# Decode attention with a gated MLP: the K and V caches loaded head by head, with the lines of a head dealt to the partitions in turn

## The chip, the core and the metric

One core of one Trainium2 chip runs the kernel. The metric is the device time of one execution in microseconds (us). Before the change it is 1299.86 us, the median of three runs (1299.61 to 1300.03).

## The reference, cut to what matters

Two tokens (B = 2, one query position each) attend to caches of 32 heads with 8192 positions of 128 float32 values. The result passes through an output projection and is multiplied by the SiLU of a small MLP.

```python
def _A_ref(x, k_cache, v_cache, wq, wo):          # k_cache, v_cache: (2, 32, 8192, 128)
    q = (lambda x, *d: x.transpose(*d))((x @ wq).reshape(B, Sq, H, Dh), 0, 2, 1, 3)
    scores = jnp.einsum("bhqd,bhkd->bhqk", q, k_cache) * (Dh ** -0.5)
    p = _softmax(scores, axis=-1)
    o = jnp.einsum("bhqk,bhkd->bhqd", p, v_cache)
    return (lambda x, *d: x.transpose(*d))(o, 0, 2, 1, 3).reshape(B, Sq, H * Dh) @ wo
...
x = A_x
xn = _layernorm(x, axis=-1)
s = _A_ref(xn, A_k_cache, A_v_cache, A_wq, A_wo)
g = _silu(_B_ref(xn, B_w1, B_b1, B_w2, B_b2))     # layernorm, 512 -> 1376, GELU, -> 512
return x + s * g
```

K and V together are 537 MB in the chip's memory (HBM), each byte used once. All other inputs are 22 MB.

## The kernel before

**Tiles.** The work goes through N = 32 pairs of heads, two heads (U = 2) at a time. The 8192 positions of a head are cut into 64 lines of KP = 128 positions; a line is 128 x 128 float32 values, 64 KB that lie together in HBM. A pair has 128 lines, and each of the 128 partitions of the on-chip memory holds one: the first head's 64 lines are on partitions 0 to 63, the second head's on 64 to 127, in the order in which they lie in HBM. `kf[n]` and `vf[n]` are the views of the caches for pair `n`, `[128 lines, 128 positions, 128 values]`.

**Buffers.** There are three of 8 MB: `KBUF[0]` and `KBUF[1]` (the tiles `big0` and `big1`) take the K of even and odd pairs, `VB` (`big2`) takes every V. At the start the weights of the query projection and of the MLP stand in `big1` and `big2`, at the end the output weights `wo` in `big2`; the last pair's V goes to `KBUF[0]`.

**A pair's way.** VectorE multiplies all of a K buffer by the query in place (`TENSOR_TENSOR`, 128x16384) and sums over the 128 values (`TENSOR_REDUCE`). TensorE moves the maximum of each head to where it is wanted, ScalarE takes the exponential into `PZ`, and TensorE multiplies `PZ` by V in 32 steps (in `weighted`) and gathers the result. Small matmuls that nothing reads (`unread`) lie in between.

**What sets the order.** Every engine runs its own program, and semaphores that are counted up and taken down tie them together. SyncE (SP in the profile) issues all large loads, in one queue: for each pair it takes `p_k` (K has been read, the buffer is free), issues the next K, takes `p_free` (V has been read), issues the next V. VectorE takes 16 counts of `d_k0` or `d_k1` before it starts on a K buffer (in `scores`), TensorE takes 16 of `d_v` ahead of V. A load adds 16 to its semaphore when all of it is in. The last K and the last V are loaded in two halves by positions (`HALVES`), each with its own semaphore, so that work can begin on the first half.

The lines of the profile carry little here: nearly every instruction is issued through one helper and stands under L51, takes of a semaphore under L45. Instructions are told apart by tiles.

## Time and profile before

| | |
|---|---|
| median of three runs | 1299.86 us |
| profiled execution | 1299.53 us |
| its span, first to last instruction | 1298.2 us |
| VectorE busy | 1135.7 us (87%) |
| TensorE busy, matmuls | 465.6 us (36%) |
| ScalarE busy | 81.1 us (6%) |
| DMA packets of the SP queue | 559.30 MB, 99.7% of 16 engines' span |
| mean rate from HBM | 431 GB/s |

The page divides the span into 40 slices and gives for each the busy share of every engine and of the 16 DMA engines in tenths, and the GB/s that they moved. It then gives the DMA queues and the chain of work that ended last, followed back from the last instruction. A row of the timeline has its start and its length in us, the engine, the operation with the tile written and the tiles read, and in brackets how long the engine had been idle before it and what ended that. A row of a stretch has its limits, its length, the busy time of each engine with the number of instructions, the granted clock of TensorE as a share of full speed, the busy share of the DMA engines and the GB/s. A row of the DMA issues has the tile and its source, the queue, how many, the size of one, and the median time from issue to landing.

### The profile page before, as it was taken

The numbers are of one execution on the slowest core, as the hardware profiler recorded it, in microseconds if no ns is written. First come the engines' busy times: TensorE is split into PE (matmuls) and PEld (weight loads), VectorE is DVE, ScalarE is ACT, GpSimd is POOL, SyncE is SP. The second block draws the span as 40 slices with busy tenths as digits, with TensorE's granted clock in tenths as the row PEclk, the third lists the DMA queues.
The fourth block names the chain that finished last, engine by engine and source line by source line (L and its number), as shares of the span: only waits on it lengthen the run. The fifth ranks groups of instructions, "written<-read, shape, count | busy, mean of one in ns | idle before, by whom it ended". The sixth has DMA issues, their size and how long they took to land. (4 is left out here: it accounts for less than half of the span.)

```text
span 1298.2 us, 7420 instructions
## 1 busy us (share of the span) xinstructions
PE 465.6 (36%) x2958; PEld 150.8 (12%) x2958; DVE 1135.7 (87%) x171; ACT 81.1 (6%) x279; POOL 2.3 (0%) x15
## 2 busy tenths in 40 slices
PE   3813343323334322433322343322334321333338
PEld 1201111001111000111100111100111100111103
DVE  2599999988889988889988888988888988888991
ACT  1200000000000000000000000000000000000000
POOL 0000000000000000000000000000000000000000
PEclk8757766666776566677656767656776666677659
DMA  9999999999999999999999999999999999999998
GB/s 412 436 426 442 430 430 436 426 446 426 438 430 424 446 426 442 430 430 436 426 446 426 438 430 424 446 426 444 428 432 434 426 446 426 438 430 424 432 436 360
DMA packets 11241, 559.37 MB, mean 431 GB/s; under 512 B 1264, under 2 KB 1536, under 8 KB 1892
## 3 DMA queue, kind: packets, MB, share of 16 engines
q1 hardware_dynamic: 11228, 559.30, 99.7%
q8 instruction: 3, 0.05, 0.0%
q14 instruction: 2, 0.02, 0.0%
q10 hardware_dynamic: 8, 0.01, 0.0%
HBM read 559.30 MB, written 0.00 MB: 431 GB/s over the span
## 5 line engine op out<-in xcount | busy, mean ns | idle before, releaser
L51 DVE TENSOR_TENSOR big<-big,bank 128x16384 f32<-128x16384 f32 (+1 forms) x33 | 551.2, 16704 | 73.2 <-DVEq L45 73.2
L51 DVE TENSOR_REDUCE sc<-big 128x128 f32<-128x16384 f32 (+1 forms) x33 | 551.2, 16703 | 4.8
L51 PE MATMUL bank<-big,PZ 128*8 128x512 f32 x2048 | 293.0, 736 | 632.1 <-PEq L45 632.1
L51 PEld LDWEIGHTS bank<-big,PZ 128*8 128x8 f32 x2048 | 60.5, 103 | 837.3 <-issue 837.3
L51 PE MATMUL bank<-Q,ident 128*128 128x512 f32 (+2 forms) x198 | 79.8, 514 | 0.3 <-issue 0.3
L51 ACT COPY o<-bank 128x512 f32<-128x512 f32 x33 | 19.3, 586 | 887.3 <-ACTq L45 875.9
L51 PE MATMUL bank<-ident,MX 128*1 128x128 f32 x32 | 9.8, 308 | 132.8 <-PEq L45 132.8
L51 PE MATMUL bank<-mod,o 128*128 128x2 f32 x256 | 32.8, 250 | 27.4 <-PEq L45 27.4
L51 PEld LDWEIGHTS bank<-mod,o 128*128 128x128 f32 x256 | 31.0, 191 | 55.4 <-issue 55.4
L51 PEld LDWEIGHTS bank<-Q,ident 128*128 128x128 f32 x198 | 34.8, 205 | 16.5 <-issue 16.5
L51 ACT ACTIVATE PZ<-sc,bias 64x128 f32<-64x128 f32 x64 | 25.5, 399 | 6.6 <-ACTq L45 6.2
L51 DVE TENSOR_REDUCE nm<-bank 1x2 f32<-1x128 f32 x32 | 8.9, 279 | 19.4 <-DVEq L45 19.4
L51 DVE TENSOR_TENSOR big<-big,mine 64x512 f32<-64x512 f32 (+1 forms) x2 | 4.5, 2278 | 21.2 <-ACT big L51 21.2
L51 PEld LDWEIGHTS bank<-ident,MX 128*1 128x1 f32 x32 | 2.5, 79 | 157.8 <-issue 157.8
L51 ACT COPY bias<-bank 128x1 f32<-128x1 f32 x32 | 5.1, 159 | 220.2 <-ACTq L45 220.2
L51 PE MATMUL bank<-big,sides 64*128 64x512 f32 x16 | 12.8, 972 | 3.7 <-DVE big L51 3.7
L51 PE MATMUL bank<-nm,srow 1*64 1x1 f32 x128 | 10.4, 218 | 8.9 <-PEq L45 7.1
L51 DVE TENSOR_REDUCE MX<-sc 128x1 f32<-128x128 f32 x32 | 9.2, 286 | 4.7
L51 PE MATMUL bank<-big,xnT 128*2 128x512 f32 x64 | 9.0, 727 | 10.3 <-DMA big<-in_A_wq_dram 10.3
L51 ACT ACTIVATION_READ_ACCUMULATOR PZ<-sc,bias x64 | 11.8, 185 | 0.0
L51 PE MATMUL bank<-big,on 128*17 128x512 f32 (+1 forms) x88 | 10.8, 569 | 0.9 <-DMA big<-in_A_wo_dram 0.8
L51 DVE SCALAR_TENSOR_TENSOR res<-bank,gate 128x128 f32<-128x128 f32 x1 | 0.3, 291 | 11.9 <-PE bank L51 11.9
(80 smaller groups left out, 83.8 us busy)
## 6 DMA issues: line engine op xcount, KB each, us to landing
big<-in_A_k_cache_dram SPq DMA_DIRECT2D x2, 4096.0 KB, 35.9
big<-in_A_v_cache_dram SPq DMA_DIRECT2D x2, 4096.0 KB, 35.8
big<-in_B_w_dram SPq DMA_DIRECT2D x1, 2752.0 KB, 10.2
big<-in_B_w_dram SPq DMA_DIRECT2D x1, 2560.0 KB, 52.1
big<-in_A_wo_dram SPq DMA_DIRECT2D x1, 2560.0 KB, 15.0
big<-in_A_wo_dram SPq DMA_DIRECT2D x1, 2048.0 KB, 19.5
big<-in_A_wo_dram SPq DMA_DIRECT2D x1, 1536.0 KB, 22.7
big<-in_A_wo_dram SPq DMA_DIRECT2D x1, 1024.0 KB, 24.8
```

Source lines behind the costliest of these rows:

```text
L51: ins = getattr(self.engines[eng], method)(*args, **kwargs)
```

## The change

Each load of a pair becomes two, one for each head. The views `kf` and `vf` get the dimensions `s` (the head of the pair), `e` (16) and `r` (4), where line 16 r + e of a head goes to partition 4 e + r of the head's 64. Before, line number and partition were the same. As the 64 partitions are divided into 16 groups of four, group e holds lines e, 16 + e, 32 + e and 48 + e; the first lines of all groups are 16 neighbours in HBM, and so are the second ones. The new `fill` issues the two loads. Who waits for a load waits for 32 counts. The sums over positions do not depend on the order of the lines, and K and V are dealt alike.

```diff
-    kf = kc.rearrange("b h s d -> (b h s d)").rearrange("(n p j d) -> n p j d", p=P, j=KP, d=DH)
-    vf = vc.rearrange("b h s d -> (b h s d)").rearrange("(n p j d) -> n p j d", p=P, j=KP, d=DH)
+    kf = kc.rearrange("b h s d -> (b h s d)").rearrange("(n s r e j d) -> n s e r j d", s=U, e=16, j=KP, d=DH, n=N)
+    vf = vc.rearrange("b h s d -> (b h s d)").rearrange("(n s r e j d) -> n s e r j d", s=U, e=16, j=KP, d=DH, n=N)
...
+    def fill(buf, src, name, c0=0, c1=KP, waits=()):
+        for s in range(U):
+            op("SP", "dma_start", buf[HP * s:HP * (s + 1), c0:c1], src[s][:, :, c0:c1], sig=name, waits=waits)
+
     def load_k(n, *waits):
         sems, cuts = ([f"d_k{n % U}", "d_kl"], HALVES) if n == N - 1 else ([f"d_k{n % U}"], (0, KP))
         for name, (c0, c1) in zip(sems, zip(cuts, cuts[1:])):
-            op("SP", "dma_start", KBUF[n % U][:, c0:c1], kf[n][:, c0:c1], sig=name, waits=waits)
+            fill(KBUF[n % U], kf[n], name, c0, c1, waits)
...
             take("SP", "p_k")
-            op("SP", "dma_start", KBUF[u], kp[i + 1, u], sig=f"d_k{u}")
+            fill(KBUF[u], kp[i + 1, u], f"d_k{u}")
             take("SP", "p_free")
-            op("SP", "dma_start", VB, vp[i, 1] if not u else vp[i + 1, 0], sig="d_v")
+            fill(VB, vp[i, 1] if not u else vp[i + 1, 0], "d_v")
...
     for i, (c0, c1) in enumerate(zip(HALVES, HALVES[1:])):
-        op("SP", "dma_start", KBUF[N % U][:, c0:c1], vf[N - 1][:, c0:c1], sig=f"d_v31{i}")
+        fill(KBUF[N % U], vf[N - 1], f"d_v31{i}", c0, c1)
...
-            take("DVE", name, 16)
+            take("DVE", name, 16 * U)
...
-            take("PE", "d_v", 16)
+            take("PE", "d_v", 16 * U)
...
-                nc.tensor.wait_ge(pr.sem(f"d_v31{HALVES.index(i * JW)}"), 16)
+                nc.tensor.wait_ge(pr.sem(f"d_v31{HALVES.index(i * JW)}"), 16 * U)
```

On SP, in the body of the loop over pairs, stood one load for each turn of a buffer. A row has the tile and its source and the destination's shape, an `ISA` row is a take of a semaphore or a step of it:

```order
L51 ISA
L51 DMA big0<-in_A_k_cache_dram 128x16384
L51 ISA
L51 DMA big2<-in_A_v_cache_dram 128x16384
L51 ISA
L51 DMA big1<-in_A_k_cache_dram 128x16384
L51 DMA big2<-in_A_v_cache_dram 128x16384
```

Now the same place on SP reads:

```order
L51 ISA
L51 DMA big0<-in_A_k_cache_dram 64x1x16384
L51 ISA
L51 DMA big0<-in_A_k_cache_dram 64x1x16384
L51 ISA
L51 DMA big2<-in_A_v_cache_dram 64x1x16384
L51 ISA
L51 DMA big2<-in_A_v_cache_dram 64x1x16384
L51 ISA
L51 DMA big1<-in_A_k_cache_dram 64x1x16384
L51 ISA
L51 DMA big1<-in_A_k_cache_dram 64x1x16384
L51 DMA big2<-in_A_v_cache_dram 64x1x16384 x2
```

Each load of 128 partitions has become two of 64, one directly behind the other in the same queue, first the lower partitions, then the upper ones. The order on the other engines is as it was.

## The prediction

> **What bounds the kernel now.** I read the page first: which resource is full in every slice, and what ended last.

> ```profile
> DMA  9999999999999999999999999999999999999998
> ...
> DMA packets 11241, 559.37 MB, mean 431 GB/s; under 512 B 1264, under 2 KB 1536, under 8 KB 1892
> ...
> q1 hardware_dynamic: 11228, 559.30, 99.7%
> ...
> DMA big<-in_A_wo_dram 2%; PE bank L51 0%; SPq L51 0%; DVE res L51 0%; DVEq L50 0%
> ```

> The 16 DMA engines are busy in every slice, 99.7% of the span, and the last thing waited for is a load. So the kernel is as long as its bytes are. VectorE has 87% in the page's first part and looks like a second bound; the timeline of one steady pair of heads shows how it really stands. Here are VectorE's rows, then TensorE's, then SP's issues:

> ```profile
> 424.05 17.22 DVE L51 TENSOR_TENSOR big<-big,bank 128x16384 f32<-128x16384 f32 x1 [2.80 <-DVEq L45]
> 441.42 17.22 DVE L51 TENSOR_REDUCE sc<-big 128x128 f32<-128x16384 f32 x1
> ...
> 462.75 17.22 DVE L51 TENSOR_TENSOR big<-big,bank 128x16384 f32<-128x16384 f32 x1 [2.84 <-DVEq L45]
> ```

> ```profile
> 443.40 9.27 PE L51 MATMUL bank<-big,PZ 128*8 128x512 f32 x64 [21.63 <-PEq L45]
> 453.56 1.02 PE L51 MATMUL bank<-mod,o 128*128 128x2 f32 x8 [0.88 <-PEq L45]
> ```

> ```profile
> 383.15 0.33 SPq L51 DMA_DIRECT2D big<-in_A_k_cache_dram  x1
> 416.02 0.33 SPq L51 DMA_DIRECT2D big<-in_A_v_cache_dram  x1
> 421.97 0.33 SPq L51 DMA_DIRECT2D big<-in_A_k_cache_dram  x1
> 454.07 0.33 SPq L51 DMA_DIRECT2D big<-in_A_v_cache_dram  x1
> ...
> 532.03 0.33 SPq L51 DMA_DIRECT2D big<-in_A_v_cache_dram  x1
> ```

> VectorE starts a K buffer at 424.05, TensorE a V buffer at 443.40, VectorE the next K at 462.75: something lands every 19.35 us, one load behind the other. Each of the two engines stands idle just ahead of its start (2.84 us on VectorE, 21.63 on TensorE), so both wait for loads. The loads do not wait for them: V is issued at 416.02, 8.0 us before the K load ahead of it is through (424.05), and the next K at 421.97, while that V has still to run. The queue is never empty.

> Sizes and landing times are in the part on issues; the whole loads are two such halves:

> ```profile
> big<-in_A_k_cache_dram SPq DMA_DIRECT2D x2, 4096.0 KB, 35.9
> big<-in_A_v_cache_dram SPq DMA_DIRECT2D x2, 4096.0 KB, 35.8
> ...
> big<-in_A_k_cache_dram SPq DMA_DIRECT2D x31, 40.7
> big<-in_A_v_cache_dram SPq DMA_DIRECT2D x31, 27.9
> ```

> One load is 8192 KB = 8.389 MB. From the V issue at 416.02 to the one at 532.03 three pairs of loads pass: 116.01 / 3 = 38.67 us for 16.777 MB, 433.9 GB/s, or 19.33 us for a load. The 64 loads of K and V take 64 x 19.33 = 1237 us of the profiled execution's 1299.53 us (its span is 1298.2; the runs' median, 1299.86, is 0.33 above, which I neglect). Some 62 us are left for the weights, the start and the end.

> **Is there something to gain in the reading?** If memory set the rate, neighbouring addresses could help, and one would expect the rate to move with the place read. Six stretches of three pairs each, start to start:

> ```profile
> 416.02:532.03 116.01, 38.92 (x250) 12.27 (x250) 104.92 (x13) 6.47 (x24) 0.00 (x0) 0.66 1.00 433
> 532.03:648.18 116.15, 39.03 (x252) 12.45 (x251) 105.06 (x13) 6.47 (x24) 0.00 (x0) 0.66 1.00 433
> ...
> 996.35:1112.50 116.15, 38.79 (x252) 12.49 (x251) 105.07 (x13) 6.47 (x24) 0.00 (x0) 0.66 1.00 433
> ```

> ```profile
> 21.00:40.00 19.00, 9.04 (x64) 1.65 (x64) 0.74 (x5) 0.26 (x3) 0.00 (x0) 0.64 1.00 435
> ```

> Through 700 us of the caches the period stays at 116.00 to 116.16 us, and in the stretch from 21 to 40 us, with other addresses, the last column reads 435 GB/s. This is a fixed ceiling, not a memory that answers better or worse. Even at 435 everywhere 1237 us shrink by 0.25%, 3 us. So the reading order is worth 0 to -3 us, and I take 0.

> **The change part by part.**

> *The lines' order.* Every line is still 64 KB in one piece and goes to one partition; sums over the lines do not depend on their order, as K and V are dealt alike. Nothing on VectorE, TensorE or ScalarE is added or moved: 0 us.

> *Twice as many loads.* 66 whole or half loads become 132. Each issue takes SP 0.33 us (the rows above), 66 x 0.33 = 22 us in all on SP's queue, which waits most of the time. V's second piece is issued some 0.4 us after the first, 7.6 us ahead of need instead of 8.0: hidden by the K load in progress. K is issued 21 us ahead of need. What the 16 engines need to close a load with its signal has no row of its own, but small loads of the output weights, issued one behind the other, bound it:

> ```profile
> 1266.60 3.65 SPq L51 DMA_DIRECT2D big<-in_A_wo_dram  x8
> ...
> big<-in_A_wo_dram SPq DMA_DIRECT2D x1, 1024.0 KB, 24.8
> big<-in_A_wo_dram SPq DMA_DIRECT2D x1, 512.0 KB, 25.6
> big<-in_A_wo_dram SPq DMA_DIRECT2D x1, 256.0 KB, 25.7
> ```

> Issued 3.65 / 8 = 0.46 us apart, the second lands 1.26 us after the first, the third 0.56 after the second. Their bytes alone need 1.21 and 0.60 us at 433.9 GB/s. Closing a load therefore costs 0.05 us at most: 66 x 0 to 0.05 = 0 to 3 us. I take 0.5.

> *Both halves awaited.* VectorE and TensorE wait for 32 counts in place of 16. They start when the second half is in, which is when the whole load would have been: 0 us.

> *64 partitions at a time.* This is the term that decides. Every large load of before is 128 partitions wide. A load of one head writes partitions 0 to 63 only, and the next one 64 to 127, behind it in the same queue. The order of instructions shows the destination as 64 rows and the source as 16 neighbouring lines, so all 16 engines can take part, four lines each. What is the ceiling of 433.9 GB/s, then? If it is what the 16 engines can carry (27.1 GB/s each), a half takes 9.67 us and the pair of halves 19.33: 0 us. If it is what the partitions can take in (433.9 / 128 = 3.39 GB/s each, in groups that share an entrance), 64 of them take 217 GB/s, two engines stand at each entrance, and a half takes 19.33 us: the 64 loads take 1237 us more. Both readings fit every row, as no large row has another number of engines or of partitions. The one narrower load, 96 partitions, is too small to tell (192 KB in 4.1 us, nearly all of it the way to the first byte):

> ```profile
> big<-in_B_w_dram SPq DMA_DIRECT2D x1, 192.0 KB, 4.1
> ```

> So the bounds are 0 and +1237 us. I take the upper end, less a little. What all rows have in common is the full width of 128 partitions; no row shows 64 of them taking in more than their half of the rate, and the loads come strictly one after the other, so the two halves do not fill each other's gap. Less a little: where the engines are not quite level, the first ones are already writing the other half; at one issue's 0.33 us for each of 128 borders that is 42 us. It is an estimate. The compute cannot get in the way: VectorE's 104.92 / 3 = 35.0 us a pair fit twice into 77.

> The sum: 1299.5 + 1237 - 42 + 0.5 = **2,495 us**.

> [...]

> **The rivals.**

> *Not slower: the engines are the ceiling.* Place: the same term. For it: 433.9 GB/s is equally 16 times 27.1, and the stretches are as even as an engine's own clock would make them. Against it: nothing in the rows. It decides as soon as an entrance takes more than two engines bring, 54 GB/s. Then the time is 1299.5 + 0.5 = 1,300 us, within 0.2%, which is about what a measurement of this kernel can tell from no change.

> *Partly slower: the engines fall out of step.* At half rate a pair of engines shares an entrance only while both are in the same half. If one gets ahead by a whole half (four lines, 9.67 us of its own time), they write different halves and the loss is gone. The queue holds one to two loads, so such a lead has room, but the queue then runs about 2 us short before each V issue (8.0 us ahead of need against 9.67). With a share f of the time in step the time is 1300 + 1237 f: 1,920 us at one half. For it: nothing holds the engines level. Against it: nothing in the rows pushes them apart either, and every short queue lets the rear catch up.

> *Faster by neighbouring reads.* Bounded above at 3 us: 1,297 us. [...]

> **How the numbers follow.** Half the rate throughout, 2,495 us: 0.45, with a range of its own from 2,400 to 2,545 (1299.5 + 1237 + 3 and a few us more). Partly out of step, 1,303 to 2,400: 0.24. Engines as the ceiling, no change: 0.25. Slightly slower by a late V alone, up to 1,330: 0.03. Faster: 0.03. Slower is 0.45 + 0.24 + 0.03 = 0.72. The two ends hold so much each that the range has to span both: 1,297 to 2,545.

> **What would show it.** In the profile after: at half rate the GB/s of the slices falls to some 220 in the steady part, while the DMA share stays full; a K or V half lands every 19 us, VectorE's idle ahead of its multiply grows from 2.8 to some 40 us, and the issues on SP lie 77 us apart. If the engines are the ceiling, every one of these stays, with 0.33 us rows doubled on SP. Out of step, the rate starts near 220 and climbs from slice to slice. The prediction is wrong if the rate stays above 300 GB/s.

## The result: twice the time

The changed kernel takes 2636.28 us (median of six runs, 2618.94 to 2653.71) against 1299.82 us before (1299.61 to 1300.43): a ratio of 2.029, 95% interval 2.025 to 2.034. The direction and the halved rate of the forecast held, its size did not: 2,495 us was said and 2,545 us was the top of the range. The profiled execution took 2618.94 us.

The page after, with the lines that answer to those of before: the slices' busy shares and rates, the queue, the chain.

```profile
span 2617.2 us, 7584 instructions
...
DVE  2735553345533355433555334554335553345550
...
DMA  9999999999999999999999999999999999999997
GB/s 300 230 208 209 211 208 211 210 211 211 209 209 210 209 210 212 211 209 209 210 210 212 213 209 211 208 211 215 210 211 210 212 212 211 210 213 215 209 215 212
...
q1 hardware_dynamic: 12284, 559.30, 99.4%
...
DMA big<-in_A_wo_dram 2%; PE bank L51 0%; SPq L51 0%; DVE res L51 0%; DVEq L50 0%
```

The busy share of the DMA engines is as full as before (99.4% against 99.7%), and a load still ends the chain. What has changed stands one line below: from the third slice on the same busy engines move 208 to 215 GB/s in place of some 434. A busy share says that packets are on their way, not how fast.

The steady part, first VectorE's timeline (start, length, and in brackets the idle time ahead), then two rows of TensorE between them in time, then SP's issues:

```profile
760.79 17.22 DVE L51 TENSOR_TENSOR big<-big,bank 128x16384 f32<-128x16384 f32 x1 [26.45 <-DVEq L45]
778.16 17.22 DVE L51 TENSOR_REDUCE sc<-big 128x128 f32<-128x16384 f32 x1
795.52 0.29 DVE L51 TENSOR_REDUCE MX<-sc 128x1 f32<-128x128 f32 x1
813.42 0.28 DVE L51 TENSOR_REDUCE nm<-bank 1x2 f32<-1x128 f32 x1 [17.61 <-DVEq L45]
841.07 17.22 DVE L51 TENSOR_TENSOR big<-big,bank 128x16384 f32<-128x16384 f32 x1 [27.37 <-DVEq L45]
```

```profile
800.89 8.53 PE L51 MATMUL bank<-big,PZ 128*8 128x512 f32 x64 [66.12 <-PEq L45]
...
812.99 0.27 PE L51 MATMUL bank<-ident,MX 128*1 128x128 f32 x1
```

```profile
250.04 1.18 SPq L51 DMA_DIRECT2D big<-in_A_v_cache_dram  x2
253.55 1.28 SPq L51 DMA_DIRECT2D big<-in_A_k_cache_dram  x2
329.60 1.26 SPq L51 DMA_DIRECT2D big<-in_A_v_cache_dram  x2
...
410.65 1.18 SPq L51 DMA_DIRECT2D big<-in_A_v_cache_dram  x2
```

VectorE's work is the same (17.22 us each), but it starts a K buffer every 80.28 us, not every 38.7. Its idle time is spread over two places: 26 to 27 us ahead of the multiply (K is not in) and 18 us ahead of `nm`. For `nm` it needs TensorE, which works off the V of the pair before first; that V is late too, so the matmul with `MX` begins only at 812.99. From 250.04 to 410.65 us two pairs pass: 80.3 us a pair for 16.777 MB, 209 GB/s.

One more number, from the trace's packets, carries the rest of this text. A line of 64 KB is one packet (each of the two traces has 7,936 of 65,536 bytes for the K and V that are loaded whole), and its duration is recorded. The table has the lines of K and V that are loaded whole:

| kernel | mean of a line, us | median, us |
|---|---|---|
| before | 2.422 | 2.422 |
| after | 4.975 | 5.032 |

Before, 8.389 MB in 128 lines over 16 engines are 8 x 2.42 = 19.4 us, the time of a load. Now each engine needs more than twice as long for the same line. Twice 2.418, the fastest of before, would be 4.84.

### The profile page after: what moved, and what is told of

Same layout as the page of the kernel before. It is cut to its first block, busy times and chain, and to the rows that moved or that the text cites. A ratio compares the mean times of both kernels' runs of the same rounds, so it can differ in the third digit from the quotient of the medians.

```text
span 2617.2 us, 7584 instructions
## 1 busy us (share of the span) xinstructions
PE 451.6 (17%) x2958; PEld 147.5 (6%) x2958; DVE 1135.8 (43%) x171; ACT 81.0 (3%) x279; POOL 2.3 (0%) x15
## 3 DMA queue, kind: packets, MB, share of 16 engines
q1 hardware_dynamic: 12284, 559.30, 99.4%
HBM read 559.30 MB, written 0.00 MB: 214 GB/s over the span
## 5 line engine op out<-in xcount | busy, mean ns | idle before, releaser
L51 DVE TENSOR_TENSOR big<-big,bank 128x16384 f32<-128x16384 f32 (+1 forms) x33 | 551.2, 16704 | 816.6 <-DVEq L45 816.6
L51 PE MATMUL bank<-big,PZ 128*8 128x512 f32 x2048 | 289.3, 728 | 2055.5 <-PEq L45 2038.4
L51 DVE TENSOR_REDUCE sc<-big 128x128 f32<-128x16384 f32 (+1 forms) x33 | 551.2, 16703 | 4.8
L51 DVE TENSOR_REDUCE nm<-bank 1x2 f32<-1x128 f32 x32 | 8.9, 279 | 575.8 <-DVEq L45 575.8
L51 PEld LDWEIGHTS bank<-big,PZ 128*8 128x8 f32 x2048 | 59.6, 102 | 2258.0 <-issue 2240.1
L51 ACT COPY o<-bank 128x512 f32<-128x512 f32 x33 | 19.3, 585 | 2305.6 <-ACTq L45 2295.7
L51 PE MATMUL bank<-Q,ident 128*128 128x512 f32 (+2 forms) x198 | 75.0, 495 | 0.3 <-issue 0.3
L51 PE MATMUL bank<-mod,o 128*128 128x2 f32 x256 | 32.8, 250 | 27.4 <-PEq L45 27.4
L51 PEld LDWEIGHTS bank<-mod,o 128*128 128x128 f32 x256 | 31.0, 191 | 55.4 <-issue 55.4
L51 PEld LDWEIGHTS bank<-Q,ident 128*128 128x128 f32 x198 | 32.4, 191 | 27.2 <-issue 27.2
L51 ACT ACTIVATE PZ<-sc,bias 64x128 f32<-64x128 f32 x64 | 25.5, 399 | 6.6 <-ACTq L45 6.2
L51 DVE TENSOR_TENSOR big<-big,mine 64x512 f32<-64x512 f32 (+1 forms) x2 | 4.5, 2279 | 22.4 <-ACT big L51 22.4
L51 PE MATMUL bank<-big,sides 64*128 64x512 f32 x16 | 12.9, 980 | 3.7 <-DVE big L51 3.7
L51 PE MATMUL bank<-ident,MX 128*1 128x128 f32 x32 | 8.8, 276 | 20.8 <-PEq L45 20.8
L51 ACT ACTIVATION_READ_ACCUMULATOR PZ<-sc,bias x64 | 11.8, 184 | 0.0
L51 DVE TENSOR_REDUCE MX<-sc 128x1 f32<-128x128 f32 x32 | 9.1, 286 | 4.7
L51 PE MATMUL bank<-nm,srow 1*64 1x1 f32 x128 | 9.0, 196 | 11.6 <-PEq L45 11.6
L51 PE MATMUL bank<-big,xnT 128*2 128x512 f32 x64 | 8.9, 721 | 11.5 <-DMA big<-in_A_wq_dram 11.5
L51 DVE RECIPROCAL rl<-bank 128x2 f32<-128x2 f32 x1 | 0.2, 170 | 23.0 <-PE bank L51 23.0
L51 PE MATMUL bank<-big,on 128*17 128x512 f32 (+1 forms) x88 | 9.1, 484 | 1.0 <-DMA big<-in_A_wo_dram 0.9
L51 ACT COPY bank<-Q 128x128 f32 (+1 forms) x34 | 9.1, 269 | 0.8
L51 PE MATMUL bank<-big,hT 128*2 128x512 f32 (+1 forms) x22 | 5.3, 1049 | 17.4 <-DMA big<-in_B_w_dram 17.4
## 6 DMA issues: line engine op xcount, KB each, us to landing
big<-in_A_wo_dram SPq DMA_DIRECT2D x1, 1024.0 KB, 42.0
```

The costliest lines, as they stand in the source:

```text
L51: ins = getattr(self.engines[eng], method)(*args, **kwargs)
```

## The experiments

**Theory "entrance".** A supposition, drawn up to be tested: the engines share their ways into the partitions, called entrances here, one of which passes about what one engine brings; partitions 0 to 63 have half of them, to go by the rates (209 against 434 GB/s), so that two engines stand at each. Entrances stand in no row; what the runs can show is the rate and the time of a line for each choice of partitions and of source. **Rivals:** "reading" (16 neighbouring lines at a time come out of HBM slowly), "count" (twice as many loads cost it), "width" (the rate goes by the number of partitions of a load, wherever they lie), and for the 100 us beyond the doubling, anything but the sharing. The diffs show the lines that decide; arguments that stay the same and the counts that are waited for are not repeated.

### The halves without the dealing

```diff
-    "(n s r e j d) -> n s e r j d"      # the view of K and V in the change
+    "(n s p j d) -> n s p j d"
```

> Two loads of 64 partitions for each pair, as in the change, but the lines lie in the order of memory (line = partition). Theory 'entrance' (partitions 0 to 63 reach half of the entrances, two engines at each): the dealing is without effect, 2,540 to 2,650 us. Rival 'reading' (16 neighbouring lines at a time are read slowly): 1,300 us. If the reading is only the part beyond the doubling (2,636 less 2,537), this kernel takes 2,537 us.

Measured: 2649.20 us (2648.27 to 2662.46), ratio 2.040 (2.035 to 2.046). The dealing is no cause of the loss; the halves alone make it. The mean line takes 5.055 us (median 5.116), and the sum goes up: 512 lines for each engine x 5.055 = 2,588, and 62 for the rest, 2,650 us. The part beyond the doubling is there without dealing too.

### Twice as many loads at full width

```diff
+        m = (c0 + c1) // 2
+        for a, b in ((c0, m), (m, c1)):
+            op("SP", "dma_start", buf[:, a:b], src[:, a:b], sig=name, waits=waits)
```

> Two loads for each pair, each 128 partitions wide and half of the columns (lines cut into two pieces of 32 KB). Theory 'entrance': full width, full rate, 1,300 to 1,303 us. Rival 'count' (twice as many loads cost the time): near 2,600 us. If closing a load costs the part beyond the doubling, 66 more loads cost 100 us: 1,400 us.

Measured: 1305.61 us (1305.26 to 1306.37), ratio 1.0043 (1.0028 to 1.0058). "Count" falls: the number of loads is that of the change, and the time is 5.6 us above before, 2 us more than the range allowed. Even these have another source, for a piece of 32 KB takes 1.217 us on the mean, two of them 2.434 and 12 ns more than a line in one piece: 512 x 12 ns = 6 us. Nothing is left for closing the loads.

### The dealing at full width

```diff
-    "(n s r e j d) -> n s e r j d"
+    "(n r e j d) -> n e r j d", e=16, r=8      # one load of 128 partitions
```

> One load of 128 partitions for each pair, with the lines dealt: line 16 r + e to partition 8 e + r, so that 16 neighbouring lines are read at a time. The heads are mixed on the partitions, so the output is another one. Rival 'reading': 2,500 to 2,650 us. [...]

Measured: 2647.79 us (2647.43 to 2648.15), ratio 2.036 (2.032 to 2.040): full width, and yet the full loss; the mean line takes 5.052 us, against 2.422 at the full width of before. Taken alone this speaks for "reading", or for engines that get in each other's way at full width too. The next one separates them.

### The same division of the partitions, other lines

```diff
-    "(n r e j d) -> n e r j d", e=16, r=8
+    "(i e u r j d) -> i u e r j d", e=16, r=8  # a group's 8 lines are neighbours, groups lie 1 MB apart
```

> One load of 128 partitions, the source in 16 groups of 8 lines as in the dealt full-width load, but each group of 8 partitions reads 8 neighbouring lines of its own, 1 MB apart from the next group's (lines 16 e + 8 h + r of two pairs of heads; the heads are mixed on the partitions, so the output is another one). [...] Rival 'reading' (16 neighbouring lines at a time are slow): 1,300 us.

Measured: 2643.04 us (2637.15 to 2648.93), ratio 2.034 (2.023 to 2.044); the mean line takes 5.056 us. Each group of 8 partitions reads 8 neighbouring lines of its own, as the rival would like, and nothing gets better: "reading" as it was put, 16 neighbouring lines at a time, falls. These two runs alone do not exclude a reading that is slow at both distances, 64 KB and 1 MB; but both come to the line time of the halves in order (5.055 us), and the next section shows that the place in the on-chip memory is enough for that. What the two slow full-width kernels share, and before has not, is a source whose first dimension has 16 entries: 5.052 and 5.056 us a line with 16, 2.422 with 128. That this dimension divides a load among the engines fits the quarters further on, where one of 8 entries has them busy for 51.2%. That 16 entries make engines meet is the author's guess; which partitions an engine wrote is in no row.

### Only the lower half, only the middle

These two decide about "width": the same number of partitions, bytes and loads, at another place. If the number sets the rate, both have the same line time.

```diff
-        for s in range(U):
-            op("SP", "dma_start", buf[HP * s:HP * (s + 1), c0:c1], src[s][:, :, c0:c1], sig=name, waits=waits)
+        op("SP", "dma_start", buf[0:64, c0:c1], src[0:64, c0:c1], sig=name, waits=waits)     # lower
+        op("SP", "dma_start", buf[32:96, c0:c1], src[32:96, c0:c1], sig=name, waits=waits)   # middle
```

> Only the lines of partitions 0 to 63 are loaded, one load of 64 partitions in the order of memory for each K and V; the other 64 partitions are set to zero once and left so, and the second head of each pair isn't computed. Half of the bytes. Theory 'entrance': a line takes 5.0 us, a load 20.1, a pair 40 us, more than VectorE's 35 to 36, so DMA still bounds: 62 + 64 x 20.1 = 1,350 us. If it were the doubled loads and not the 64 partitions, a pair's loads take 19.3 us and VectorE bounds, 1,200 to 1,250 us.

> As the one before, with the same number of partitions, bytes and loads, but partitions 32 to 95; 0 to 31 and 96 to 127 are set to zero once and left so, and those halves of the heads aren't computed. [...] Rival 'width' (64 partitions are half as fast wherever they lie): 1,350 us as the lower ones.

Measured: lower 1373.05 us (1370.49 to 1375.62), middle 1265.47 us (1264.80 to 1266.14). From the two pages the queue and the rates, and from the DMA issues the median time from issue to landing; first the lower partitions:

```profile
GB/s 381 236 199 205 211 209 197 209 211 197 207 211 207 199 209 211 195 209 211 207 199 209 211 193 211 211 207 199 207 213 193 211 211 207 197 209 211 192 210 285
...
q1 hardware_dynamic: 7004, 290.86, 99.7%
...
big<-in_A_k_cache_dram SPq DMA_DIRECT2D x31, 45.0
big<-in_A_v_cache_dram SPq DMA_DIRECT2D x31, 30.1
```

then the middle ones, and behind them two rows of VectorE's timeline:

```profile
q1 hardware_dynamic: 7004, 290.86, 56.0%
...
big<-in_A_k_cache_dram SPq DMA_DIRECT2D x31, 12.3
big<-in_A_v_cache_dram SPq DMA_DIRECT2D x31, 12.3
```

```profile
692.87 17.22 DVE L51 TENSOR_TENSOR big<-big,bank 128x16384 f32<-128x16384 f32 x1
...
729.08 17.22 DVE L51 TENSOR_TENSOR big<-big,bank 128x16384 f32<-128x16384 f32 x1 [0.25 <-DVEq L45]
```

### Three pieces: the middle and two quarters

```diff
+        for a, b in ((32, 96), (0, 32), (96, 128)):
+            op("SP", "dma_start", buf[a:b, c0:c1], src[a:b, c0:c1], sig=name, waits=waits)
```

> Three loads for each pair in the order of memory: partitions 32 to 95 first, then 0 to 31, then 96 to 127. [...] Rival 'width' (the rate goes by the number of partitions in a load): 19.33 us for each of the three, 58 a load, 3,774 us. Rival 'reading': 1,300 us.

Measured: 2418.03 us (2400.89 to 2435.18), ratio 1.860 (1.844 to 1.875). Neither of the two numbers was met. In the first two K loads the middle runs at the line time of full width and each quarter at about twice that; the medians of consecutive groups of 32 lines, in us:

```
2.42  2.42  5.02  4.99     first K: middle, middle, lower quarter, upper quarter
2.42  2.43  5.03  4.98     second K
```

A group of 32 lines is two for each of 16 engines, so the first load adds up to 2 x (2.42 + 2.42 + 5.02 + 4.99) = 29.7 us. With 62 us for the rest, 64 such loads would take 62 + 64 x 29.7 = 1,963 us, an estimate. It was not met either: the pieces run into one another. The page:

```profile
DMA  9999989788998888988889879789797799797994
GB/s 335 299 268 269 237 194 253 195 224 209 222 250 214 222 227 193 259 231 197 226 205 253 237 198 242 221 212 268 224 224 210 197 250 253 198 240 209 208 253 167
...
q1 hardware_dynamic: 13340, 559.31, 87.7%
```

The engines are idle for 12% of the time, and a few hundred lines take over 5.6 us, some 7.4, about three times 2.42. That engines which finish a quarter late disturb the next middle piece is a guess; why it costs as much as 455 us above 1,963 was not settled. In the profiled run, which took 2435.18 us, the idle engines account for some 300 of the 472 us (12.3% of 2433.1 us); the rest stands in lines that take longer.

### Quarters, over 16 engines and over 8

```diff
-    "(n s r e j d) -> n s e r j d", s=U, e=16
+    "(n s r e j d) -> n s e r j d", s=4, e=16, r=2    # 2 lines for each of 16 engines
+    "(n s r e j d) -> n s e r j d", s=4, e=8, r=4     # 4 lines for each of 8 engines
...
+        for s in range(4):
+            op("SP", "dma_start", buf[32 * s:32 * (s + 1), c0:c1], src[s][:, :, c0:c1], sig=name, waits=waits)
```

> Four loads of 32 partitions for each pair, the lines dealt over 16 engines (2 lines each). [...] Rival 'width' (the rate goes by the number of partitions): a quarter of the rate, 1300 + 3 x 1237 = 5,010 us.

> Four loads of 32 partitions for each pair, the lines dealt over 8 groups of 4 partitions, so that 8 engines take part and each has an entrance of its own. Theory 'entrance': half of the engines do as much as all 16 with quarters; without sharing a line takes its 2.42 us again, and the part beyond the doubling (2,636 less 2,537) is gone: 2,537 us and 1 to 10 us for 200 more loads. If the time beyond the doubling comes from elsewhere (reading, or the number of loads): 2,630 us and more. Rival 'engines' (the rate is what the engines carry, and sharing was not the cause): 2,537 us too, but then the quarters over 16 engines take 1,300.

Measured: over 16 engines 2634.19 us (2616.82 to 2651.55), over 8 engines 2548.55 us (2547.98 to 2549.12), ratio 1.961 (1.955 to 1.967). The page of the quarters over 8 engines:

```profile
DMA  7544544544544544544545545545545545545457
GB/s 324 217 215 214 221 215 215 220 215 215 220 215 215 220 215 216 220 214 216 220 214 217 219 214 218 218 214 218 218 214 219 217 214 219 217 214 219 212 218 224
...
q1 hardware_dynamic: 12284, 559.30, 51.2%
```

32 partitions over 16 engines are as fast as 64 (2634.19 against 2636.28 us), not half as fast: "width" falls once more. And half of the engines (51.2% busy) do more than all of them: with eight on 32 partitions a line is through in 2.419 us on the mean, as fast as at the full width of before (2.422). So the part beyond the doubling is the price of sixteen engines sharing what eight can fill. In the halves in order, with sixteen, a line takes 5.055 us by the mean and 5.116 by the median in place of 4.84, some 4 to 6% longer than twice the time. With eight the time is 11.5 us above 2,537, a little more than the 1 to 10 us allowed for 200 more loads. Their lines are dealt too, eight neighbours at a time, and 2.419 against 2.422 us is all that the reading order brings.

### The two halves in two queues

```diff
             take("ACT", "p_n")
+            for buf, src, name in k_loads:                                 # upper half of K
+                op("ACT", "dma_start", buf, src, sig=name)
...
             take("ACT", "p_t")
+            if v_load is not None:
+                op("ACT", "dma_start", VB[HP:], v_load, sig="d_v")         # upper half of V
```

> The loads of the change, but from the third pair on the upper half of each buffer is issued by ScalarE, so that lower and upper half stand in two queues. Theory 'entrance': the loss comes from all engines being in the same half. If an engine with both queues filled keeps both halves moving, all entrances are in use and the time returns most of the way, 1,300 to 1,700 us; if the engines take lines from the two queues in turn and stay in step, 2,640 us stays. A theory by which 64 partitions a load are slow as such gives 2,640 us.

Measured: 2393.47 and 2574.15 us in two runs. The slices of the faster one:

```profile
GB/s 311 226 219 214 224 219 225 222 228 228 222 228 227 224 233 230 231 229 228 230 230 233 235 228 229 232 239 231 238 236 241 241 238 242 242 244 253 238 236 249
```

Neither expectation: the rate starts near 220 and climbs to some 245 by the end, and the two runs lie 7% apart. It looks like the third case of the forecast, engines that fall out of step little by little, only too slowly to help; no row shows which engine stood where, so this is not shown, and two runs so far apart give no size. The mean line of this run is 4.55 us.

## Why the prediction was right or wrong

- **The bound.** Right. DMA bounds before and after, and VectorE's 35 us a pair fit into the longer period.
- **Nothing to gain in the reading.** Right: without dealing and with it a line takes 2.422 us (before, full width) and 2.419 (the quarters over 8 engines). In halves over 16 engines 5.055 and 4.975 us were measured in one run each, but the medians of the two kernels lie only 13 us apart and their runs overlap.
- **Twice as many loads, 0.5 us.** Right in kind: the full-width kernel with as many loads loses 5.6 us, which its shorter lines explain. The bound of 0.05 us for closing a load was finer than its rows, which give landing times to 0.1 us; nothing of the 5.6 us is left for it.
- **64 partitions at a time.** The choice between the two bounds was right. The rows of before could not make it, as the prediction says, so that at 0.45 against 0.25 there was luck in it. Of the two readings of 433.9 GB/s the one by partitions held. "Width" as the prediction put it (3.39 GB/s for each partition) was loose; it is the place of the partitions that counts, for the median line takes 2.420 us in 32 to 95 and 5.116 in 0 to 63. That entrances are the reason was not shown; that the engines share a limit was: on 32 partitions at a time eight took 2548.55 us and sixteen 2634.19. The upper bound itself is the step that failed: it let two engines that share pass their lines in exactly twice the time of one, 19.33 us a half and +1,237 us, and called that the end: a price of the sharing itself stood in the sum at nothing, without a reason. The trace measured 4.975 us a line and 2618.94 us, so K and V took (2618.94 - 62) = 2,557 us, +1,320. Sharing has a price of its own; the quarters over 8 engines, without sharing, come to 2,549 and so nearly to the old bound. Of the 141 us between 2,495 and the median some 99 are this price and 42 the deduction that follows.
- **Less 42 us for engines that are not level.** Not shown in size. Line times well below the 5.116 us median of the halves in order are there (the mean after is 4.975), so some lead may exist. If 5.116 were the pace in step, it would be worth 512 x 0.141 = 72 us in the profiled run; but the first lines of that run, before any lead could grow, already have medians of 5.03 to 5.09 us. What is clear is that the deduction took the forecast further from the result: without it, it would have been 2,537, still 4% short.
- **The narrower load of 96 partitions.** Misread, but it decided nothing: the 4.1 us of its 192 KB are not nearly all the way to the first byte. In the trace its first packet starts 1.0 us after the issue, and its last ends 3.4 us after it.
- **The rivals.** "Engines as the ceiling" fell with the result. "Out of step" did not come about in one queue: the rate goes from 208 to 215 GB/s over the whole run. With two queues the rate climbs as this rival says, without being shown to be its work.
- **What would show it.** Rate said 220, found 208 to 215; a period of 77 us said, 80.3 found; some 40 us of idle time on VectorE said, 26 and 18 found, in two places.

## What to carry to other kernels

A full busy share of the DMA engines does not say which end of the path is full: it was 99.7% at 2.422 us a line and 99.4% at 4.975, so look at the time of one line. Compare places and divisions before loads are narrowed: here the median line took 2.420 us with partitions 32 to 95 and 5.116 with 0 to 63, and at full width the mean line took 2.422 us with a source whose first dimension has 128 entries and 5.052 to 5.056 with 16. Price a shared resource by more than its share: here lines of sixteen engines on 64 partitions took 4 to 6% longer than twice the time.

## What was not expected of the hardware

- A load of all 128 partitions became twice as slow by its source's view alone: 2,643 to 2,648 us with a first dimension of 16, in both orders of lines that were tried, 1,300 us with one of 128.
- Eight DMA engines moved 212 to 221 GB/s through the steady slices and took 2,549 us, where sixteen on the same partitions took 2,634.
- Lines cut into pieces of 32 KB cost 12 ns a line, 5.6 us in all.
- The order in which lines are read made no difference that can be seen: 2.42 us a line in the order of memory over sixteen engines and with neighbours dealt to eight.
